# Two batches of attention back to back with their own PSUM buffers, then MLP steps alone while the third batch loads

## The chip, the cores and the metric

The kernel runs on one core of a Trainium2 chip. Its core has five instruction queues: TensorE (PE, matrix products), VectorE (DVE), ScalarE (ACT), GpSimd (POOL) and SyncE (SP). Here POOL and SP also issue the DMA transfers, POOL the loads and SP the transposing copies and the stores. PE writes into PSUM, eight banks of 128 x 512 fp32; everything else lies in SBUF. The metric is the time of one execution on the device in microseconds (us), less being better; a kernel is known by the median of its runs.

## What is computed

Attention with a decay ("forgetting") term over 8 batches of 8 heads, 576 positions, 64 features a head; its output, 4608 rows of 512, goes through an MLP whose activation is h - tanh(h). Cut to what matters:

```python
scores = np.matmul(q, k.transpose(0, 1, 3, 2)) / np.sqrt(D)      # 8 x 8 x 576 x 576
cum    = np.cumsum(np.log(np.clip(f, 0.0001, 1.0)), axis=-1)
decay  = cum[:, :, :, None] - cum[:, :, None, :]
scores = np.where(causal, -1e9, scores + decay)                  # causal: column after row
attn   = softmax(scores)
x      = np.matmul(attn, v).transpose(0, 2, 1, 3).reshape(4608, 512)
h      = x @ w_in                                                # 512 -> 2048
out    = (h - np.tanh(h)) @ w_out                                # 2048 -> 512
```

Matrix operands are fp16 (converted by the loads), sums are fp32.

## The kernel before

**Attention.** The heads go in 32 pairs (b, c): batch b, heads 2c and 2c+1. Each pair has its *slot* p = 4b + c, in which its scores are computed while the pair before gets its values. Scores are computed transposed, keys on the partitions, in seven tiles (`TILES`): three of 512 columns for each head, and one of 128 columns (`LAST`) that both heads share. A tile is one to three matmuls into a PSUM bank (L287) and an exponential on ACT into SBUF (L301), cut at the causal edge either by a matmul that adds a large negative triangle (L295, "early" slots 0 to 3) or by a select on POOL (L311). Values are 30 matmuls of 65 columns (L322), 15 a head, normalised on DVE (L332 to L334). `turn` (L338) then transposes the pair's output into `XR`, the input of the MLP: batch 0 on PE with a copy by ACT or DVE, later batches by two transposing DMAs of SP (L352, L354).

**Operands.** `QT` and `KT` hold q and k with the features on the partitions (rows 0 to 63) and three further rows that bring in the decay: constant rows (`const_rows`, L174) and rows of the cumulative logs (`load_aug`, L168), all written by SP's DMAs. There are two of each, for even and odd batches. For batches 0 and 1 q and k are loaded by `load_qk` (L84), six positions of a head in a row (1536 bytes of DRAM), turned on PE (`trans`, L242) and copied out of PSUM with a stride of 2 (L260, L262). From batch 2 on `load_block` (L89) loads blocks of 128 positions, `turn_block` (L94) turns each by a transposing DMA on SP (five for q into `TQ`, five for k into `TK`), and `place` (L98) copies the result into `QT` or `KT` on DVE. In slot 0 two tiles are computed *direct*, without the three rows, adding the decay by two matmuls with `pick_k` and `pick_q` (L290, L292).

**MLP.** 4608 rows are 9 units of 512. A unit begins with 16 steps `mlp1` (L369): four matmuls of 512 columns (`hps`, L366), tanh on ACT (L373), `gt` = h + tanh(-h) on DVE (L379). In units 1 to 8 the second product is computed as seven products of half size (`product`, L394; 14 steps of eight 256-column matmuls), which need four differences of blocks of `w_out` (`wsum`, L233) and sums of blocks of `gt` (`sums`, L383), all on DVE; `settle` (L423) adds partial results and issues the stores on SP (L435). Unit 0 takes the plain product instead, 16 steps `mlp2` (L438) of four 512-column matmuls. That is 16 + 16 + 8 x 30 = 272 steps.

**Order.** Everything is emitted in an order written out by hand, and `manual_schedule` keeps program order on all five engines. Slots 0 to 4 follow the lists `BEGIN`, `ORDER` and `THEN` (L454 to L456): s is a score tile, va and vb values, q and k transpositions for a later pair, x is `turn`, a number is so many filler matmuls (`spin`). Later slots run their seven tiles with the values after tile 1. `take` (L520) says how many MLP steps are spread over a slot: none in slots 0 to 3, 3 in slot 4, then 7 or 8. `LOADS` (L198 to L225) attaches loads, transposing DMAs and placings to a tile of a slot. What the slots leave of the MLP follows alone at the end.

**PSUM** is in four pools for the whole program: scores 2 banks (`ps_sc`), values 2 (`ps_av`), 1 shared (`ps_tr`), and 3 (`ps_m`) for the transpositions of the start and for the MLP.

Of the kernel before, what the change touches and what calls it, by code (L numbers as in the profile page):

```python
# [22 lines left out]
def kernel(  # L23
# [31 lines left out]
    aex = ctx.enter_context(tc.tile_pool(name="aex", bufs=10))  # L55
# [6 lines left out]
    ps_sc = ctx.enter_context(tc.tile_pool(name="ps_sc", bufs=2, space=PSUM))  # L62
    ps_av = ctx.enter_context(tc.tile_pool(name="ps_av", bufs=1, space=PSUM))
    ps_tr = ctx.enter_context(tc.tile_pool(name="ps_tr", bufs=1, space=PSUM))
    ps_m = ctx.enter_context(tc.tile_pool(name="ps_m", bufs=3, space=PSUM))
# [62 lines left out]
    pick_k = WS[3].rearrange("p k e -> p (k e)")[:, 0:512]  # L128
    pick_q = cst.tile([P, P], FP16)
# [4 lines left out]
    EL = [cst.tile([P, 192], FP16, tag=f"el{i}", name=f"el{i}") for i in range(3)]  # L134
    nc.vector.memset(id16, 0.0)
# [5 lines left out]
    nc.vector.memset(minus16, -1.0)  # L141
    nc.vector.memset(neg16, 0.0)
    nc.vector.memset(tri16, 0.0)
    nc.gpsimd.affine_select(out=neg16, in_=neg16, compare_op=ALU.not_equal,
# [3 lines left out]
    for i in range(2):  # L148
        nc.vector.memset(KT[i][:, :, S:PITCH], 0.0)
    nc.vector.memset(pick_k, 0.0)  # L150
    nc.vector.memset(pick_q, 0.0)
    nc.vector.memset(cqs[NH:P, :], 0.0)
    nc.vector.tensor_scalar(out=lf, in0=lf, scalar1=0.0001, scalar2=1.0,
                            op0=ALU.max, op1=ALU.min)
    nc.scalar.activation(out=lf, in_=lf, func=AF.Ln)
    nc.vector.memset(pick_k[0:1, :], -1.0)
    nc.vector.memset(pick_q[0:1, :], 1.0)
# [5 lines left out]
    nc.scalar.activation(out=cq, in_=cum, func=AF.Copy, bias=-SHIFT * inv_qscale, scale=inv_qscale)  # L163
    nc.vector.scalar_tensor_tensor(out=clo, in0=cum, scalar=inv_qscale, in1=chi,
                                   op0=ALU.mult, op1=ALU.subtract)
    nc.vector.memset(pick_k[NH:NH + 1, :], -1.0)

    def load_aug(b):  # L168
        i, h0 = b % 2, b * H
        nc.sync.dma_start(out=KT[i][D:D + 1, :, 0:S], in_=chi[h0:h0 + H, :])  # L170
        nc.sync.dma_start(out=QT[i][D + 2:D + 3, :, :], in_=cq[h0:h0 + H, :])
        nc.sync.dma_start(out=KT[i][D + 1:D + 2, :, 0:S], in_=cc[NH + h0:NH + h0 + H, :])

    def const_rows(i):  # L174
        nc.sync.dma_start(out=QT[i][D:D + 2, :, :], in_=minus16)
        nc.sync.dma_start(out=KT[i][D + 2:D + 3, :, 0:S], in_=ones16[0:H, :])

    const_rows(0)
    load_aug(0)
    const_rows(1)  # L180
    load_qk(qn, q, 0, 4, H)
    load_qk(kn, k, 0, 4, H)
    for e in EL:
        nc.gpsimd.memset(e, 0.0)
    for i in range(2):
        nc.gpsimd.memset(vn[i][D:P, NJ - 1, :, :], 0.0)
        nc.gpsimd.memset(vn[i][:, :, :, D:VW], 1.0)
    load_v(0)
# [5 lines left out]
    def load_wout(t0, t1):  # L194
# [3 lines left out]
    LOADS = {(0, 0): [lambda: load_qk(qn, q, 1, 0, 2), lambda: load_qk(kn, k, 1, 0, 2),  # L198
                      lambda: load_win(0, DFF // 2)],
             (0, 3): [lambda: load_qk(qn, q, 1, 2, H), lambda: load_qk(kn, k, 1, 2, H)],  # L200
             (1, 0): [lambda: load_v(1)],
             (1, 3): [lambda: load_win(DFF // 2, DFF)],
             (2, 0): [lambda: load_wout(0, NFT // 2)],
             (3, 0): [lambda: load_wout(NFT // 2, NFT)]}
# [4 lines left out]
    for n in range(4):  # L209
        for i in range(2):  # L210
            LOADS.setdefault((NPAIR + 3 + n, 1 + 3 * i), []).append(lambda n=n, i=i: wsum(n, i * K2 // 2, (i + 1) * K2 // 2))
    for b in range(2, B):
        p0 = (b - 1) * NPAIR
        q0, k0, v0, tq, tk = {2: (5, 10, 21, 14, 16), 3: (-2, 3, 9, 6, 12)}.get(b, (-7, 0, 7, 4, 11))
        for n in range(NJ):
            at_tile(p0, q0 + n, lambda b=b, n=n: load_block(qb, q, b, n))
            at_tile(p0, k0 + n, lambda b=b, n=n: load_block(kb, k, b, n))
            at_tile(p0, v0 + n, (lambda b=b, n=n: load_v_block(b, n, 0, H)) if n < NJ - 1 else lambda b=b: load_v_rest(b))
            at_tile(p0, tq, lambda b=b, n=n: turn_block(TQ, qb, b, n))
            at_tile(p0, tk, lambda b=b, n=n: turn_block(TK, kb, b, n))  # L220
# [16 lines left out]
    def spin(n):  # L237
        t32 = ps_tr.tile([P, UW], FP32, tag="tr", name="spin")
        for _ in range(n):
            nc.tensor.matmul(out=t32, lhsT=ones16[:, 0:P], rhs=ones16[:, 0:UW])  # L240

    def trans(b, c, src, dst, early, eng, by_head=False):  # L242
        pn, g3 = S // NT6, NT6 // 2
        if early:
            t32 = ps_m.tile([P, UW], FP32, tag="m", name="t32")
        else:
            t32 = ps_tr.tile([P, UW], FP32, tag="tr", name="t32")
        t16 = t32.bitcast(FP16)[:, 0:2 * S // 2].rearrange("p (a g n) -> p a g n", a=2, g=g3)
        for a in range(2):
            for g in range(g3):  # L250
                nc.tensor.transpose(out=t16[:, a, g, :],  # L251
# [315 lines left out]
```

## Time and profile before

| | |
|---|---|
| runs | 355.82, 356.16, 358.69 us; median 356.16 |
| the profiled execution's own time | 358.62 us |
| its span (first to last instruction in the profile) | 356.9 us |
| granted TensorE clock, mean | 0.974 |
| first scores of pair 8 (batch 2) | 74.47 us |
| last attention slot's end, MLP alone after it | about 298 us |

In the page of the profile, PE is the matmul stream and PEld its weight loads, which run beside it. A row of the chain of waits is *start, duration, engine, tile, line*; a row of a timeline the same with shapes and, in brackets, the idle time before it and what ended it. A row of a group ends in *busy us, mean ns of one, idle us before* and what ended that idle time. A row of the windows is *window, length, busy us of PE, PEld, DVE, ACT, POOL with the instructions in brackets, granted TensorE clock (1 is full), DMA share, GB/s*. SPq is SP issuing a DMA.

### The profile page before, as it was taken

How to read it: one execution, taken by the hardware profiler on the slowest of the kernel's cores; microseconds unless marked ns; L12 is line 12 of the kernel's file. 1: busy time of each engine (PE TensorE's matmuls, PEld its weight loads, DVE VectorE, ACT ScalarE, POOL GpSimd, SP SyncE). 2: the span in 40 equal slices, each digit the busy share in tenths (PEclk: the TensorE clock that was granted, in tenths of full speed). 3: DMA queues.
4: the chain of work that ended last, by engine and by line, in shares of the span. 5: the costliest groups of instructions: out<-in, count | busy, mean ns of one | idle time of the engine just before them, and what ended most of it. 6: DMA issues, size and time to landing. Idle time of an engine off the chain costs nothing.

```text
span 356.9 us, 8463 instructions
## 1 busy us (share of the span) xinstructions
PE 339.8 (95%) x3192; PEld 229.8 (64%) x3192; DVE 257.4 (72%) x501; ACT 218.8 (61%) x416; POOL 165.3 (46%) x324
## 2 busy tenths in 40 slices
PE   6698799999999999999999999999999999899995
PEld 3366455555567756887887568756887786386474
DVE  8557489963899489938893899389838855864871
ACT  6468377557775587558755875587558734533630
POOL 8941157498757755775567557753222310000000
PEclk9769889999999999999999999999999999999999
DMA  7999999999999997999799989994221112002002
GB/s 106 160 203 188 208 103 112 131 181 166 152 117 109 159 172 83 102 150 175 94 107 148 189 84 93 159 184 59 55 94 28 26 50 90 2 29 91 0 17 103
DMA packets 157469, 39.98 MB, mean 112 GB/s; under 512 B 142276, under 2 KB 155828, under 8 KB 157428
## 3 DMA queue, kind: packets, MB, share of 16 engines
q0 software_dynamic: 100128, 18.36, 70.3%
q1 hardware_dynamic: 57300, 21.09, 33.5%
q8 instruction: 25, 0.41, 0.5%
q14 instruction: 16, 0.13, 0.1%
HBM read 36.85 MB, written 9.44 MB: 130 GB/s over the span
## 4 chain that ended last, share of the span: by engine, by line
PE 79%; DVE 10%; ACT 3%; DMA 3%; SPq 2%; issue 2%; DVEq 0%; ACTq 0%
PE hps L366 29%; PE px L413 15%; PE ps L287 12%; PE pm L413 12%; PE av L322 8%; DVE gt L379 4%; PE ops L444 2%; DVE sm L392 2%; DMA QT<-cqs 2%; ACT e L301 2%; ACT th L373 2%; SPq L96 1%; DMA TK<-kn 1%; PE t L251 1%; DVE xn L334 1%
## 5 line engine op out<-in xcount | busy, mean ns | idle before, releaser
L366 PE MATMUL hps<-XR,win 128*128 128x512 f16 (+4 forms) x704 | 143.7, 344 | 2.0 <-DVE gt L379 2.0
L301 ACT ACTIVATE e<-ps 128x512 f16<-128x512 f32 x192 | 110.9, 596 | 30.5 <-PE ps L287 19.4
L373 ACT ACTIVATE th<-hps 128x512 f32<-128x512 f32 x144 | 86.3, 599 | 53.4 <-PE hps L366 47.1
L379 DVE TENSOR_TENSOR gt<-hps,th 128x512 f16<-128x512 f32 x144 | 96.7, 686 | 23.7 <-ACT th L373 22.1
L311 POOL TENSOR_SCALAR_AFFINE_SELECT e<-e 128x128 f16<-128x128 f16 x168 | 62.4, 373 | 107.8 <-ACT e L301 107.4
L366 PEld LDWEIGHTS <-win 128*128 128x128 f16 x704 | 62.4, 98 | 53.4 <-issue 7.2
L287 PE MATMUL ps<-QT,KT 67*128 67x64 f16 (+5 forms) x384 | 77.8, 285 | 5.1 <-DMA QT<-cqs 2.7
L287 PEld LDWEIGHTS <-KT 67*128 67x128 f16 (+1 forms) x384 | 37.5, 100 | 28.8 <-issue 6.4
L413 PEld LDWEIGHTS <-gt 128*128 128x128 f16 x512 | 48.0, 97 | 10.2 <-DVE gt L379 1.3
L413 PEld LDWEIGHTS <-sm 128*128 128x128 f16 x384 | 36.1, 97 | 5.4
L322 PEld LDWEIGHTS <-e 128*128 128x128 f16 x896 | 33.0, 98 | 5.6 <-issue 1.7
L322 PE MATMUL av<-vn,e 128*128 128x65 f16 x896 | 34.8, 195 | 1.3 <-DVE xn L334 1.0
L434 DVE TENSOR_TENSOR ost<-pm,part 128x512 f32<-128x512 f32 x24 | 16.5, 686 | 22.7 <-PE pm L413 8.2
L428 ACT ACTIVATE part<-px 128x512 f32<-128x512 f32 x24 | 14.3, 597 | 30.1 <-PE px L413 30.1
L413 PE MATMUL pm<-ws,gt 128*128 128x256 f16 x256 | 32.2, 272 | 0.0
L413 PE MATMUL px<-ws,sm 128*128 128x256 f16 x256 | 31.5, 272 | 0.0
L110 POOL DMA_DIRECT2D vn<-in_v_dram x32 | 28.4, 889 | 2.5 <-issue 1.4
L332 DVE TENSOR_SCALAR rs<-av 128x10 f32<-128x10 f32 (+1 forms) x33 | 5.3, 160 | 32.2 <-PE av L322 32.2
L334 DVE TENSOR_TENSOR xn<-av,rs 128x640 f16<-128x640 f32 (+1 forms) x33 | 26.5, 804 | 1.3 <-DMA out_dram<-ost 0.2
L91 POOL DMA_DIRECT2D qn<-in_q_dram x30 | 25.9, 864 | 2.1 <-issue 1.8
L91 POOL DMA_DIRECT2D kn<-in_k_dram x30 | 25.5, 849 | 1.4 <-issue 1.2
L413 PE MATMUL pm<-wout,gt 128*128 128x256 f16 x128 | 17.2, 273 | 0.2 <-DVE gt L379 0.2
(74 smaller groups left out, 291.9 us busy)
## 6 DMA issues: line engine op xcount, KB each, us to landing
out_dram<-ost SPq DMA_DIRECT2D x36, 256.0 KB
vn<-in_v_dram POOLq DMA_DIRECT2D x32, 128.0 KB, 6.3
qn<-in_q_dram POOLq DMA_DIRECT2D x24, 128.0 KB, 4.0
kn<-in_k_dram POOLq DMA_DIRECT2D x24, 128.0 KB, 5.1
win<-in_moe_w_in_dram POOLq DMA_DIRECT2D x2, 1024.0 KB, 11.8
wout<-in_moe_w_out_dram POOLq DMA_DIRECT2D x2, 1024.0 KB, 17.1
XR<-xn SPq DMA_TRANSPOSE x56
vn<-in_v_dram POOLq DMA_DIRECT2D x8, 64.0 KB, 6.9
```

The source lines that it names most:

```text
L91: nc.gpsimd.dma_start(out=dst[b % 2][0:pn, n, :].rearrange("p (h d) -> p h d", h=H), in_=src[b, :, n * P:n * P + pn, :].rearrange("h p d - ...
L110: nc.gpsimd.dma_start(out=vn[b % 2][:, n, h0:h1, 0:D], in_=v[b, h0:h1, n * P:(n + 1) * P, :].rearrange("h p d -> p h d"))
L287: nc.tensor.matmul(out=ps[:, col:col + n], lhsT=KT[b % 2][0:rows, h, j * P:(j + 1) * P], rhs=QT[b % 2][0:rows, h, i0:i0 + n], start=True, ...
L301: nc.scalar.activation(out=e[:, lo:hi], in_=ps[:, lo:hi], func=AF.Exp, scale=qscale)
L311: nc.gpsimd.affine_select(out=view, in_=view, compare_op=ALU.is_ge, fill=0.0, base=0, pattern=pat, channel_multiplier=-1)
L322: nc.tensor.matmul(out=av[:, a, ib, :], lhsT=E.pop((b, c, a, j, ib)), rhs=vn[b % 2][:, j, 2 * c + a, 0:D + 1], start=(j == 0), stop=(j == ib))
L334: nc.vector.tensor_tensor(out=xn[:, :, h0 * D:(h0 + hn) * D].rearrange("p i (a d) -> p a i d", a=hn), in0=av[:, h0:h0 + hn, :, 0:D], in1=r ...
L366: nc.tensor.matmul(out=hps[:, o:o + n], lhsT=win[:, ci, ft * P:(ft + 1) * P], rhs=XR[:, ci, t:t + n], start=(ci == 0), stop=(ci == NCH - 1))
L373: nc.scalar.activation(out=th, in_=hps, func=AF.Tanh, scale=-1.0)
L379: nc.vector.tensor_tensor(out=GT[(u, ft)], in0=hps, in1=th, op=ALU.add)
L413: nc.tensor.matmul(out=ps[:, g * E2:(g + 1) * E2], lhsT=left(k), rhs=right[:, k, :], start=(first and g == 0 and k == 0), stop=(k == K2 - ...
L434: nc.vector.tensor_tensor(out=ost, in0=ps, in1=PART.pop((u, {2: 1, 7: 5, 4: 6}[n])), op=ALU.add)
```

## The change

- **Loads.** `load_qk` takes the positions in rows of 96: the pieces are 256 bytes of DRAM, and the copies out of PSUM write runs of 96 columns instead of every second one. All loads of batches 0 and 1 (q and k in pieces of two heads), then `w_in` in four quarters and `w_out` in two halves, are issued one after the other on POOL's queue ahead of slot 0, not at tiles of slots. Batch 2's loads ("b") follow at the start of slot 7.
- **Start.** Three tiles (those of head 0) are direct; the two broadcast operands are one tile `pick` of two columns. Memsets of pads move from POOL and the prologue to DVE inside slot 0 ("p", "r"). The decay rows of batch 0 are loaded for heads 1 to 7 only, those of batch 1 in slot 0, those of batch 2 and head 0's constant rows in slot 4 ("c").
- **Slots 0 to 6.** Slot 0 has a pool of four one-bank buffers; slots 1 to 6 one of two two-bank buffers, into which tiles go in groups (0,1), (2,4), (5,6), (LAST), each with one exponential of up to 1024 columns. The transpositions alternate between two banks. No MLP step stands in these slots. Causal edges are cut by PE's matmul in slots 0 to 7. `turn` uses SP's transposing DMAs for all pairs but pair 3.
- **Slots 7 and 8.** The pools of before are opened from slot 7 on (2 banks of scores, 3 of MLP). Slot 7 holds four MLP steps among its tiles. Slot 8 starts with the values of pair 7, 18 + 12 steps alone, and batch 2's transposing DMAs and placings between them, and only then come pair 8's scores.
- **MLP.** `mlp2` and the split of a step (`mlp1_part`) are gone: all nine units take 16 + 14 steps, 270 in all. The weight differences stand in unit 0, behind its steps 14, 16, 19 and 21. From slot 8 on `take` is 5 for slots 8 to 11, 6 for 12, then 7 or 8.

SP's order after the change, from pair 7's output on: two transposing DMAs of pair 7, the store of product 2 of unit 0 (step 21), five of q, the store of product 7 (step 25), five of k.

The core of the diff:

```diff
     def load_qk(dst, src, b, h0, h1):
         nc.gpsimd.dma_start(
-            out=dst[b % 2][:, h0:h1, :, :].rearrange("p h n d -> p h (n d)"),
-            in_=src[b, h0:h1, :, :].rearrange("h (p n) d -> p h (n d)", n=NT6))
+            out=dst[b % 2][:, h0:h1, :, :].rearrange("p h n d -> p (h n) d"),
+            in_=src[b, h0:h1, :, :].rearrange("h s d -> (h s) d").rearrange("(m p) d -> p m d", p=S // NT6))
...
+    for h in (0, 2, 4):
+        load_qk(qn, q, 1, h, h + 2)
+        load_qk(kn, k, 1, h, h + 2)
+    load_v(1)
+    load_qk(qn, q, 1, 6, H)
+    load_qk(kn, k, 1, 6, H)
+    for i in (0, 2, 1, 3):
+        load_win(i * QW, (i + 1) * QW)
+    for i in range(2):
+        load_wout(i * NFT // 2, (i + 1) * NFT // 2)
...
-                to = dst[b % 2][0:D, h0:h0 + an, e:S:2].rearrange("d a (p g) -> d a p g", g=g3)
-                of = t16[e * D:(e + 1) * D, a0:a0 + an, :, :].rearrange("d a g p -> d a p g")
+                to = dst[b % 2][0:D, h0:h0 + an, 0:S].rearrange("d a (g e p) -> d a g e p", g=g3, e=2)[:, :, :, e, :]
+                of = t16[e * D:(e + 1) * D, a0:a0 + an, :, :]
...
+    GROUPS = [(0, 1), (2, 4), (5, 6), (LAST,)]
...
+        banks = POOLS["s"].tile([P, 2 if how == "group" else 1, UW], FP32, tag="sc", name="ps")
...
+        nc.scalar.activation(out=eb[:, :, lo:hi], in_=banks[:, 0:n2, lo:hi], func=AF.Exp, scale=qscale)
...
+    for at, n in ((NFT - 2, 0), (NFT, 2), (NFT + 3, 1), (NFT + 5, 3)):
+        mlp[at] += [(wsum, n, 0, K2 // 2), (wsum, n, K2 // 2, K2)]
...
+    FIRST = [["8", "q0", "k0", "5", "q1", "4", "s0", "s1", "k1", "p", "s2", "s4", "s5", "q2", "r", "s6", "s3"],
+             ["g0", "g1", "k1", "g2", "va", "vb", "q2", "x", "g3"],
+             ["g0", "va", "g1", "k1", "vb", "g2", "q2", "x", "g3"],
+             ["g0", "va", "g1", "k1", "vb", "g2", "q2", "x", "g3"],
+             ["c", "g0", "va", "g1", "k1", "vb", "g2", "x", "q2", "g3"],
+             ["g0", "g1", "k1", "g2", "va", "vb", "x", "g3"],
+             ["g0", "va", "g1", "q1", "vb", "x", "g2", "k1", "g3"],
+             ["b", "s0", "va", "s1", "vb", "m", "s2", "x", "m", "s3", "s4", "m", "s5", "m", "s6"],
+             ["va", "m", "vb", "m", "x"] + ["m"] * 16 + ["tq"] + ["m"] * 4 + ["tk"] + ["m"] * 4 + ["pq"] + ["m"] * 4 + ["pk"]]
...
+        with tc.tile_pool(name="ps_t2", bufs=1, space=PSUM) as POOLS["t"]:
+            with tc.tile_pool(name="ps_one", bufs=4, space=PSUM) as POOLS["s"]:
+                first_slot(0)
+            with tc.tile_pool(name="ps_two", bufs=2, space=PSUM) as POOLS["s"]:
+                for p in range(1, 2 * NPAIR - 1):
+                    first_slot(p)
...
+            take = 5 if p < 3 * NPAIR else 6 if p == 3 * NPAIR else 8 - p % 2
```

In `FIRST`, m is an MLP step, s a tile, g a group, tq and tk the five transposing DMAs of q and k of batch 2, pq and pk their placing.

More of the change, by code (lines that the diff above doesn't have):

```diff
@@ L303, in scores @@
             return
+        ti, e = tis[0], eb[:, 0, :]
         col, cp, step, wd = MASKS[ti]
@@ L507 @@
[L507 to L513 removed]
+    pairs = [(b, c) for b in range(B) for c in range(NPAIR)]
+    turns = [o + 2 * i + e for i in range(K2 // 2) for o in (0, K2) for e in range(2)]
@@ L536 @@
                     given += 1
-        for fn, *args in mlp[at:]:
-            fn(*args)
+        while STEPS[0] < len(mlp):
+            step()
 _INS = ['q', 'k', 'v', 'f', 'moe_w_in', 'moe_w_out']
```

403 lines of the change are left out of this document (194 added, 209 removed).

## The prediction

> **What bounds the kernel now.** I read first the page, then the windows cut at 74.47 (the start of pair 8's scores, the first of batch 2), then the chain of waits before that cut, the groups by form, and last the timelines of the start and of one early slot.
>
> ```profile
> PE 339.8 (95%) x3192; PEld 229.8 (64%) x3192; DVE 257.4 (72%) x501; ACT 218.8 (61%) x416; POOL 165.3 (46%) x324
> ...
> 0.00:74.47 74.47, 64.24 (x587) 37.50 (x587) 53.80 (x98) 45.28 (x86) 42.76 (x80) 0.89 1.38 151
> 74.47:297.78 223.31, 222.51 (x2255) 158.06 (x2256) 165.61 (x333) 149.66 (x291) 122.49 (x245) 1.00 1.17 117
> ```
>
> TensorE (PE) is 95% busy. From 74.47 on it idles 0.80 us of 223.31, so that stretch is PE work and nothing else. Of the first 74.47 us it is busy 64.24. The change rewrites that first stretch and renames work in the second, so the forecast is a forecast of when pair 8's scores start, and of how many MLP steps are done by then.
>
> ```profile
> 63.83 1.23 SPq L354
> ...
> 65.16 6.52 SPq L96 DMA_TRANSPOSE TK<-kn  x5
> 80.84 0.53 SPq L450 DMA_DIRECT2D out_dram<-ost  x1
> 81.47 6.60 SPq L96 DMA_TRANSPOSE TQ<-qn  x5
> ...
> 70.42 3.23 DMA TK<-kn
> 73.86 0.56 DVE KT L99
> 74.47 0.61 PE ps L287 x3
> 75.94 0.90 PE av L322 x30
> ...
> 87.18 0.86 PE hps L366 x4
> 108.22 0.88 PE px L413 x8
> ```
>
> The chain of waits says what starts pair 8 today: SyncE's queue (SPq) finishes the transposition of pair 7's output, issues five block transpositions of k (x5 in 6.52, so 1.30 each; 6.60 for q's five later), the last lands after 3.23, VectorE (DVE) places it (0.56), PE starts. A store costs the queue 0.53. Pair 7's values come only afterwards (0.90). Four matmuls of an mlp1 step take 0.86, eight of a product 0.88: 0.87 a step.
>
> **The exchange rate.** Before, 24 of 272 steps are done at 74.47, 248 are left, and the values. After, the slots list puts 4 steps in slot 7 and 30 in slot 8 ahead of pair 8, of 270: 236 are left and no values. That is 12 x 0.87 + 0.90 = 11.3 less. So pair 8 may start at 74.47 + 11.3 = 85.8 and the end stays where it is. All below asks whether it starts sooner.
>
> **Start (slot 0).**
>
> ```profile
> 7.46 1.99 ACT L260 ACTIVATE QT<-t 64x288 f16<-64x288 f16 x4
> 14.38 0.42 PE L287 MATMUL ps<-QT,KT 67*128 67x320 f16 x1 [2.74 <-DMA QT<-cqs]
> 18.36 0.59 PE L287 MATMUL ps<-QT,KT 67*128 67x512 f16 x1 [0.47 <-ACT e L301]
> 7.50:10.00 2.50, 1.52 (x11) 0.67 (x12) 2.41 (x5) 1.90 (x5) 2.44 (x6) 1.00 1.07 133
> 12.50:15.00 2.50, 0.62 (x5) 0.53 (x6) 0.86 (x2) 0.00 (x0) 2.50 (x5) 0.76 2.48 154
> ```
>
> PE's first scores wait for q's four copies on ScalarE (ACT), 7.46 to 9.45, and the rows of decay cost another idle 2.74 until 14.38. The change lets only head 0 go without these rows (3 tiles in place of 2) and places q1's transposition, which needs the bank that those copies free, before the scores: first scores about 9.27 + 0.9 = 10.2, the three direct tiles to 12.7, the rows (three DMAs fewer ahead of them) between 12.7 and 14.4. Slot 1 then begins at 16.5 where it began at 18.36; bounds 14.5 (rows hidden) and 18.4 (no gain). The q and k loads go from 1536-byte to 256-byte pieces. The row at 12.50 holds v's 256-byte pieces at 154 GB/s, the row at 7.50 q's long ones at 133: no loss taken.
>
> The Trainium skill, "DMA: Bandwidth & Descriptors", Specifications, puts the smallest transfer for full rate at 512 bytes; by it the new loads are slower than the old, and rival 4 below would hold. The 154 against 133 GB/s here does not agree.
>
> **Slots 1 to 6.**
>
> ```profile
> L301 ACT ACTIVATE e<-ps 128x512 f16<-128x512 f32 x192 | 110.9, 596 | 30.5 <-PE ps L287 19.4 <-PE ps L295 8.1 <-POOL e L311 1.4
> L301 ACT ACTIVATE el<-ps 128x128 f16<-128x128 f32 x32 | 8.9, 278 | 2.6 <-PE ps L287 2.1 <-PE ps L295 0.2
> L262 DVE COPY QT<-t 64x576 f16<-64x576 f16 x14 | 11.2, 800 | 4.7 <-PE t L251 4.5
> L348 DVE COPY XR<-x 128x576 f16<-128x576 f16 x1 | 0.5, 458 | 2.6 <-PE x L346 2.6
> 28.39 0.38 PE L287 MATMUL ps<-QT,KT 67*128 67x512 f16 x1
> 28.60 0.22 PE L295 MATMUL ps<-ws 128*128 128x128 f16 x1
> 28.92 0.60 ACT L301 ACTIVATE e<-ps 128x512 f16<-128x512 f32 x1 [0.41 <-PE ps L295]
> 29.94 2.52 ACT L301 ACTIVATE e<-ps 128x512 f16<-128x512 f32 x4
> 33.31 0.38 PE L287 MATMUL ps<-QT,KT 67*128 67x512 f16 x1
> ```
>
> A slot lasts 33.31 - 28.39 = 4.92 now; ACT runs four exponentials in 2.52, 0.63 each. From 128 columns (278 ns) to 512 (596) a column costs 0.83 ns, so 1024 take 0.596 + 512 x 0.83 ns = 1.02. New ACT work of a slot: 3 x 1.02 + 0.28 = 3.34. But there are two buffers of two banks: the next slot's first group (1280 columns with its two edges; 512 take 0.21 from 28.39 to 28.60, so 0.53) can be written only after the third group is read, while ACT has only the 0.28 exponential to do. With the lag from the start of PE's last write to ACT (28.60 to 28.92, 0.32) ACT idles 0.53 + 0.32 - 0.28 = 0.57, and I add 0.33 for a lag at one more group, where values stand on PE between two groups: 4.24 for slots 2, 3, 4 and 6, and 4.0 for 1 and 5, whose values come after the third group: 25.0. Ends: 3.34 and 4.92 each. DVE does not bind: its copies become contiguous (between 458 and 800 ns, near 480), four a slot, plus 1.25 for normalising: 3.2. So slot 7 begins at 16.5 + 25.0 = 41.5 (36.5 to 46).
>
> **What costs nothing here, and its cover.**
>
> ```profile
> L186 POOL MEMSET vn<- 64x528 f16 x2 | 1.3, 692 | 0.1
> L149 DVE MEMSET KT<- 67x256 uint32 x2 | 0.5, 272 | 0.0
> ```
>
> Seven memsets (three of KT, four of vn) go to DVE in slot 0, at most 3 x 0.27 + 4 x 0.69 = 3.6. They lie where DVE was busy 0.14 of 3.41 (13.80:17.21, under Clock); without that cover q2's copies, and so slot 2, would be later by as much. The transposition of pairs 0 to 2's output moves from PE and ACT to SyncE, two issues each, in an almost empty queue; the first MLP step is the first to need it, some 15 us later. Edges of slots 4 to 7 go from GpSimd to PE: eight of 128 columns, at 0.21 for 512, are 0.42 a slot, beside a bound on ACT. The 5 spins fewer are filler. Unit 0's 16 mlp2 steps of four 512-column matmuls become 14 products of eight 256-column ones, counted in the 270. Batch 3's plan moves by less than a slot, inside the stretch where PE idles 0.80.
>
> **Slot 7 and the first MLP steps.**
>
> ```profile
> L373 ACT ACTIVATE th<-hps 128x512 f32<-128x512 f32 x144 | 86.3, 599 | 53.4 <-PE hps L366 47.1 <-DVE gt L379 4.0 <-DVE rs L333 1.1
> L379 DVE TENSOR_TENSOR gt<-hps,th 128x512 f16<-128x512 f32 x144 | 96.7, 686 | 23.7 <-ACT th L373 22.1
> L392 DVE TENSOR_TENSOR sm<-gt 128x512 f16<-128x512 f16 x32 | 13.9, 435 | 1.1
> L235 DVE TENSOR_TENSOR ws<-wout 128x1024 f16<-128x1024 f16 x4 | 2.8, 706 | 0.0
> L434 DVE TENSOR_TENSOR ost<-pm,part 128x512 f32<-128x512 f32 x24 | 16.5, 686 | 22.7 <-PE pm L413 8.2 <-ACT e L301 6.3 <-issue 5.1
> 304.18 3.61 PE L366 MATMUL hps<-XR,win 128*128 128x512 f16 x16 [0.34 <-DVE gt L379]
> 40.00:45.00 5.00, 3.38 (x29) 1.86 (x28) 2.70 (x4) 1.34 (x4) 1.00 (x3) 0.84 1.24 208
> ```
>
> Slot 7 has six exponentials, the short one and four tanh on ACT: 6 x 0.63 + 0.31 + 4 x 0.63 = 6.6, so slot 8 begins at 48.1. Its values take 0.90 and the 11 steps to the fifteenth mlp1 step 11 x 0.86, with 0.34 of idle for every four (row 304.18), about 1.3 with the start: 59.8. Batch 2's loads stand behind the weights on GpSimd's queue: 3.5 MB of batches 0 and 1 at 154 GB/s is 23, 4.2 MB of weights at 208 is 20, so weights are in by 46 and batch 2 by 58. They wait for nobody and nobody waits for them.
>
> What is late is the queue of SyncE. It issues in order, and in the new order the store of product 2 (step 21) stands ahead of the five transpositions of q, the store of product 7 (step 25) ahead of the five of k. The first store waits for DVE, which after the fifteenth step's gt does, in this order, weight sums 1.41 (two of 0.71), gt 0.69, two sums 0.87, 1.41, four in-place sums 1.74, 1.41, 0.43, and the store's addition 0.69: 8.7, from 59.8 + 1.6 (tanh, gt). Store ready 70.1; q's transpositions from 70.9 to 77.5; a store 0.6; k's four spacings 5.2, landing 2.7 (the one shown 3.23, shorter when its queue is empty), wake and first copy 0.76: pair 8 at 86.8. PE gets its second weight sums (product 6) at 65.8, ends product 2 three steps later at 68.4, and then has eight products and four mlp1 steps, 10.5: it stands still some 8 us in all, part of it before the last of the four, since the gt of these steps stand behind the placing of q on DVE. Ends: 81.4 if DVE or the slots are 5 us ahead, 92 if both are behind.
>
> **Clock.**
>
> ```profile
> 10.39:13.80 3.41, 1.25 (x10) 0.51 (x7) 2.94 (x4) 1.09 (x2) 3.41 (x5) 1.00 1.96 165
> 13.80:17.21 3.41, 2.68 (x18) 1.79 (x19) 0.14 (x1) 1.73 (x3) 2.59 (x5) 0.50 2.18 157
> 34.28:37.70 3.42, 1.88 (x35) 1.30 (x32) 1.62 (x4) 2.25 (x5) 0.29 (x1) 1.00 1.17 207
> 37.70:41.11 3.41, 3.41 (x19) 1.60 (x16) 0.85 (x3) 1.19 (x2) 0.69 (x2) 0.50 1.24 210
> ```
>
> A window with PE 1.25 of 3.41 busy is followed by one at 0.50, and one with 1.88 too. After a stall of 8 us at least one window at half clock follows: 3.41/2 = 1.7 of work lost. Ends 0 and 5.1 (three windows). The same may befall slots 1 to 6, where the upper end of 46 has room for it. I take 1.7: 88.5. The Trainium skill, "TensorE: Matmul & The Clock Gate", Part 1, says half clock follows at least one idle window of about 3.4 us; since steps stand between the two gaps, by that rule nothing might be lost, and the time would be 1.7 less, 358.0; the rows here halve after windows only half idle, so I keep it.
>
> **Sum.** 88.5 - 85.8 = +2.7. Slots 8 to 11 have five steps: ACT 6 x 0.60 + 0.28 + 5 x 0.60 = 6.88 while these are mlp1, against PE's 3200 columns 1.31 + 0.90 + 5 x 0.87 = 6.56; the first 12 of the 20 steps are mlp1, two slots and a half: +0.8 (0 to 1.6). The tail (last 60 steps alone) has the same 0.34 gaps as now. Together +3.5: the span goes from 356.9 to 360.4. The profiled execution took 358.62, 2.5 above the median of the runs, 356.16; the difference is carried to the median: 359.7.
>
> **Rivals.**
> 1. *Slots at ACT's pace* (the other side: not slower). If the refill is hidden, six slots take 3.34: 5.0 less, all that follows moves with it, and the time is 354.7. It decides from about 3.5 a slot. For it: ACT's spacing in 29.94 x4 is 0.03 over its work. Against: only 0.28 of exponential covers a 0.54 refill.
> 2. *The transpositions hide.* If the queue reaches q's five before the store's wait matters, or ten pass in under 8 us, the chain ends with PE's steps at 68.4 + 10.5 = 78.9: 88.5 - 78.9 = 9.6 less, 350.1. Against: every five of these in the trace took 6.5 to 6.6, in program order.
> 3. *The wide exponential does nothing*, slots stay at 4.92: +4.1, 363.8. For: DVE or PE order, not ACT, may end the waits.
> 4. *Small pieces starve the slots.* If q and k of batches 0 and 1 come at half of 154 GB/s, their 2.4 MB take 15 us more, of which the first slots' own slack hides a third: 10 later, 369.7. The row at 12.50 speaks against.
>
> **Chances.** Forecast 0.45 (357 to 363), rival 1 0.16, rival 2 0.20, rival 3 0.14, rival 4 0.05. 1% is 3.6, about what a measurement can tell from no change: below 352.6 lie rival 2 and a little of rival 1, 0.23; within it most of rival 1 and nearly half of the forecast, 0.34; above 359.7 the rest, 0.43. The range leaves out a half of rival 2 and rival 4, 0.15, and reaches from rival 2's 350 to 3 above rival 3: 350 to 366.5.
>
> **What would show it.** Slot 1 at 16.5; slots of 4.2 with ACT idle before the first wide group; wide exponentials of 1.02; the store of product 2 issued near 70 with q's transpositions right behind it; pair 8 at 87 released by a copy of KT; PE idle 8 us before it, then a window at 0.50. It is wrong if pair 8 starts before 82, or if a load or a slot, not SyncE's queue, ends the wait.

## The result, and the profile after

The changed kernel is slower: 370.27 us median (367.73 to 371.20, four runs) against 355.99, ratio 1.038 [1.030, 1.046] (here and below the bracket is the 95% interval of the ratio to the kernel before, run beside it). Forecast were 359.7 and at most 366.5. Its profiled execution took 367.73 with a span of 366.0, the quickest of its four. ACT's timeline at the start of slot 3, two wide exponentials (1.02 each; 2.10 with what lies between), 0.70 of idle before them:

```profile
24.07 2.10 ACT L339 ACTIVATE e<-ps 128x1024 f16<-128x1024 f32 x2 [0.70 <-PE ps L323]
```

SP's timeline, then DVE's, then PE's, in the stretch ahead of pair 8:

```profile
68.85 0.43 SPq L455 DMA_DIRECT2D out_dram<-ost  x1
69.39 7.53 SPq L99 DMA_TRANSPOSE TQ<-qn  x5
77.02 0.53 SPq L455 DMA_DIRECT2D out_dram<-ost  x1
77.64 6.45 SPq L99 DMA_TRANSPOSE TK<-kn  x5
```

```profile
71.34 0.69 DVE L454 TENSOR_TENSOR ost<-mb,part 128x512 f32<-128x512 f32 x1 [0.31 <-PE mb L433]
79.71 0.69 DVE L454 TENSOR_TENSOR ost<-mb,part 128x512 f32<-128x512 f32 x1 [7.68 <-DMA out_dram<-ost]
...
86.46 0.42 DVE L415 TENSOR_TENSOR sm<-sm,gt 128x512 f16<-128x512 f16 x1
86.80 1.65 DVE L102 COPY KT<-TK 64x1152 f16<-64x1152 f16 x4
```

```profile
80.45 1.87 PE L393 MATMUL mb<-XR,win 128*128 128x512 f16 x4 [4.00 <-DVE ost L454]
82.74 1.86 PE L393 MATMUL mb<-XR,win 128*128 128x512 f16 x4 [0.42 <-DVE gt L402]
87.31 1.04 PE L323 MATMUL ps<-QT,KT 67*128 67x512 f16 x3 [2.70 <-DVE KT L102]
```

Here and below the first number of a row is its start, the second its duration. Up to here the forecast holds to little more than 1 us: the store of product 2 at 68.85 (forecast 70.1), q's five transpositions right behind it, pair 8 at 87.31 (86.8), released by a copy of `KT`. Not foreseen is DVE's 7.68 of idle: its third addition needs one of two `ost` buffers, and the store that frees it (product 7) stands in SP's queue behind q's transpositions. Nor is it foreseen that k is placed straight behind the sums (86.46), with no wait for a transfer: what holds pair 8 last is DVE's program order behind that addition. Then windows of 3.41 (PE's busy time behind the length, the granted clock third from the end), and what PE waited for from 87 to 310, behind the 2.7 for `KT` (total, times, longest):

```profile
75.24:78.65 3.41, 1.21 (x6) 0.46 (x5) 0.00 (x0) 1.19 (x2) 0.00 (x0) 1.00 1.35 151
78.65:82.06 3.41, 1.61 (x4) 0.56 (x4) 2.31 (x6) 0.00 (x0) 0.00 (x0) 0.63 0.65 141
...
85.47:88.89 3.42, 1.58 (x5) 0.64 (x6) 2.90 (x7) 0.94 (x2) 0.27 (x2) 0.50 0.43 140
88.89:92.30 3.41, 3.41 (x12) 1.47 (x11) 0.69 (x1) 1.31 (x4) 3.06 (x6) 0.50 0.73 47
92.30:95.71 3.41, 3.41 (x17) 1.53 (x16) 1.47 (x3) 2.97 (x7) 2.63 (x7) 0.87 1.45 128
95.71:99.13 3.42, 3.42 (x45) 2.07 (x44) 3.11 (x7) 2.43 (x5) 3.39 (x6) 1.00 2.44 141
```

```profile
PE mb L393 <- DVE gt L402: 2.3, 5, 0.5
PE mb L393 <- DMA XR<-xn: 1.0, 1, 1.0
PE av L360 <- POOL e L350: 0.7, 2, 0.4
```

The clock is halved from about 80 to 93, and after pair 8 three kinds of waits come, where the kernel before idled 0.80 in all up to the end of its slots. One measure carries all that follows: when pair 8 starts, and the span less that. The kernel before leaves 356.9 - 74.47 = 282.4 after it; by the exchange rate of the forecast (11.3 less work) the changed kernel should leave 271.1. It leaves 366.0 - 87.31 = 278.7.

### The profile page after: what moved, and what is told of

Read it like the earlier page. It is cut to its first block, busy times and chain, and to the rows that moved or that the text cites. A ratio compares the mean times of both kernels' runs of the same rounds, so it can differ in the third digit from the quotient of the medians.

```text
span 366.0 us, 8530 instructions
## 1 busy us (share of the span) xinstructions
PE 336.7 (92%) x3266; PEld 233.5 (64%) x3266; DVE 255.4 (70%) x523; ACT 216.2 (59%) x395; POOL 163.4 (45%) x300
## 4 chain that ended last, share of the span: by engine, by line
PE 55%; DMA 16%; DVE 10%; POOL 7%; ACT 4%; SPq 4%; issue 3%; POOLq 0%; DVEq 0%; ACTq 0%
PE mb L393 20%; PE px L433 13%; PE mb L433 10%; DMA qn<-in_q_dram 8%; PE ps L323 7%; DVE gt L402 5%; PE av L360 4%; SPq L99 3%; DVE sm L415 3%; ACT th L396 3%; DMA vn<-in_v_dram 3%; DMA kn<-in_k_dram 2%; POOL kn L88 2%; POOL vn L113 2%; ACT e L339 2%
## 5 line engine op out<-in xcount | busy, mean ns | idle before, releaser
L393 PE MATMUL mb<-XR,win 128*128 128x512 f16 (+4 forms) x704 | 145.4, 346 | 10.5 <-DVE gt L402 5.5
L339 ACT ACTIVATE e<-ps 128x512 f16<-128x512 f32 (+1 forms) x174 | 107.6, 640 | 31.2 <-PE ps L323 21.1
L402 DVE TENSOR_TENSOR gt<-mb,th 128x512 f16<-128x512 f32 x144 | 97.2, 688 | 32.3 <-ACT th L396 29.7
L396 ACT ACTIVATE th<-mb 128x512 f32<-128x512 f32 x144 | 86.2, 599 | 54.4 <-PE mb L393 39.8
L323 PE MATMUL ps<-QT,KT 67*128 67x64 f16 (+4 forms) x384 | 74.4, 280 | 7.7 <-DVE KT L102 2.7
L454 DVE TENSOR_TENSOR ost<-mb,part 128x512 f32<-128x512 f32 x27 | 18.6, 688 | 53.2 <-DMA out_dram<-ost 22.3
L323 PEld LDWEIGHTS <-KT 67*128 67x128 f16 x384 | 36.4, 99 | 26.4 <-DVE KT L102 3.6
L433 PE MATMUL mb<-ws,gt 128*128 128x256 f16 x288 | 36.0, 272 | 0.0
L368 DVE TENSOR_TENSOR xn<-av,rs 128x640 f16<-128x640 f32 x32 | 26.4, 825 | 1.1
L433 PE MATMUL mb<-wout,gt 128*128 128x256 f16 x144 | 18.7, 272 | 0.0
```

Of the source, the lines that this page charges most:

```text
L323: nc.tensor.matmul(out=ps[:, col:col + n], lhsT=KT[b % 2][0:D + 3, h, j * P:(j + 1) * P], rhs=QT[b % 2][0:D + 3, h, i0:i0 + n], start=True ...
L339: nc.scalar.activation(out=eb[:, :, lo:hi], in_=banks[:, 0:n2, lo:hi], func=AF.Exp, scale=qscale)
L368: nc.vector.tensor_tensor(out=xn.rearrange("p i (a d) -> p a i d", a=2), in0=av[:, :, :, 0:D], in1=rs.to_broadcast([P, 2, NJ, D]), op=ALU. ...
L393: nc.tensor.matmul(out=hps[:, o:o + n], lhsT=win[:, ci, ft * P:(ft + 1) * P], rhs=XR[:, ci, t:t + n], start=(ci == 0), stop=(ci == NCH - 1))
L396: nc.scalar.activation(out=th, in_=hps, func=AF.Tanh, scale=-1.0)
L402: nc.vector.tensor_tensor(out=GT[(u, ft)], in0=hps, in1=th, op=ALU.add)
```

## Experiments

The theory at this point: SP's queue makes the stall, the stall halves the clock, both add up. Rivals: the loads hold pair 8; what is gained is given back later; the two profiles compared are not typical.

**1. Both kernels again (ctl_before, ctl_after).** No edit.

> The kernel before as it is, for a second profile: the one shown took 358.62, the other runs 355.12 to 356.16. Theory A: a profile at about 355.5 has one or two windows at 0.50 fewer in the first 50 us than the one shown (which has them at 13.80 to 24.04, 37.70 and 44.52) and pair 8 at about 71.5 in place of 74.47. Rival B: the same windows, and the 3 us lie elsewhere, or in the time outside the span. Ratio 1.00.

> The changed kernel as it is. Its profiled execution took 367.73, the other three 369.53 to 371.20 at a lower mean clock (0.976 against 0.981). Theory A (the slow runs differ in how long the clock stays halved): a profile at about 370 shows more windows at 0.50 than the first one, which has them only from 78.65 to 92.3, and pair 8 at about 87 again. Rival B (they differ in the transfers): the windows at 0.50 are the same and pair 8 starts 2 to 3 later, at 89 to 90. Ratio 1.03 to 1.045 either way.

Measured: 356.01 and 369.57, ratio of the second 1.039 [1.034, 1.044]. Of the second profiles, a window and PE's row of pair 8, first of before, then of the changed kernel (spans 352.2 and 368.5):

```profile
17.21:20.63 3.42, 3.42 (x49) 3.08 (x47) 1.01 (x3) 1.63 (x3) 3.42 (x5) 0.50 1.09 194
```

```profile
69.85 0.61 PE L287 MATMUL ps<-QT,KT 67*128 67x512 f16 x3 [0.25 <-DVE KT L99]
```

```profile
41.11:44.52 3.41, 1.71 (x38) 1.38 (x36) 2.07 (x6) 1.79 (x3) 1.54 (x2) 1.00 1.22 198
44.52:47.93 3.41, 3.41 (x26) 1.84 (x23) 1.63 (x4) 1.60 (x3) 0.61 (x2) 0.52 1.25 200
```

```profile
89.92 1.03 PE L323 MATMUL ps<-QT,KT 67*128 67x512 f16 x3 [2.70 <-DVE KT L102]
```

The kernel before started pair 8 at 69.85, 4.6 sooner than in the profile of the forecast, and left 352.2 - 69.85 = 282.4, the same to a tenth. The changed kernel started it at 89.92 and left 368.5 - 89.92 = 278.6, again the same. So in these profiles each kernel varies ahead of pair 8 alone. Of the 2.6 by which the changed kernel starts it later, 1.2 lie already in slot 0 (slot 1's first exponential is at 16.62 and not 15.45, slot 7's at 43.89 and not 42.73). The other 1.4 go with a window at 0.52 in slot 7, behind one only 1.71 busy; the earlier start of before goes with about three halved windows fewer. That fits theory A's cause for a part, though pair 8 moved, as rival B had it.

**2. Fillers in the gaps (spins).** `["pq", "m", "m", "16", "m", "m", "pk", "18"]` at the end of slot 8's list.

> The changed kernel with filler matmuls in the two gaps ahead of pair 8: 16 behind the second of the four last MLP steps, 18 behind the fourth. Theory A (half clock, brought on by the gaps, costs 2.9 after pair 8 starts and about 1.5 in the steps before it): no window at 0.50 from 75 on, pair 8 at 86 to 87, span 362 to 363.5, ratio 1.02 to 1.03. Rival B (the wait for the transposed k alone is what costs): pair 8 at 87.3 or later by what filler is left over, the time within 1 us of the changed kernel, ratio 1.035 to 1.045.

Measured 371.19, 1.044 [1.038, 1.049]. The clock stays at 1.00 from 52 to 129, and nothing is won: `KT` is placed from 88.32, but the fillers run over and pair 8 starts at 89.85; what is left after it is 370.9 - 89.85 = 281.1, more than with the clock halved. PE's timeline of spins shows longer waits:

```profile
120.26 0.45 PE L360 MATMUL av<-vn,e 128*128 128x65 f16 x9 [0.32 <-POOL e L350]
130.74 0.58 PE L393 MATMUL mb<-XR,win 128*128 128x512 f16 x1 [3.60 <-DMA XR<-xn]
```

The wait for pair 11's output (`XR`, which unit 2 needs) is 3.60 where ctl_after has 1.47, and values wait for selects on GpSimd; behind the 3.60 the clock falls again (a window at 0.59 from about 130). This is rival B in substance: PE only waits longer there. As the fillers ran over, the price of half clock alone isn't isolated.

**3. The order of SP's queue (queue2), DVE's buffer (inplace), both and more (q_first).**

```diff
- ... ["m"] * 16 + ["tq"] + ["m"] * 4 + ["tk"] + ["m"] * 4 + ["pq"] + ...
+ ... ["m"] * 15 + ["tq"] + ["m"] * 5 + ["tk"] + ["m"] * 4 + ["pq"] + ...    # queue2
+ ... ["m"] * 15 + ["tq", "tk"] + ["m"] * 9 + ["pq"] + ...                   # q_first
-            nc.vector.tensor_tensor(out=ost, in0=ps, in1=PART.pop(...), op=ALU.add)
+            ost = PART.pop(...)                                             # inplace, q_first
+            nc.vector.tensor_tensor(out=ost, in0=ps, in1=ost, op=ALU.add)
```

> The changed kernel with the order of SyncE's queue alone changed: five transpositions of q, the stores of products 2 and 7, then the five of k (each step stays where it was). Theory A (the order of that queue holds pair 8 back, and with it VectorE, which waits 7.7 for the store of product 7): q's transpositions start at about 64, k's at 71 to 72, VectorE does not wait for that store, pair 8 at 81 to 83, span 360 to 362, ratio 1.01 to 1.025. Rival B (the loads hold it back: k's last block of batch 2 landed at 70.2): k's transpositions move but last longer beside the loads of v, pair 8 at 85 to 87, span 364 to 366, ratio 1.03 to 1.04.

> The changed kernel with products 2, 7 and 4 added into the tile of the partial result and stored from there, so that VectorE needs no buffer that a store has to give back; SyncE's order as in the changed kernel. Theory A (VectorE, standing 6.5 to 7.7 for the store of product 7 behind q's transpositions, is a link of its own): the wait of 7.7 is gone, q is placed about 79 to 80, the third of the four MLP steps ahead of pair 8 runs at once and not after 4.0 of idle; pair 8 then waits for k's transpositions alone, 1 to 2 earlier than in the changed kernel, less half clock: 366 to 368, ratio 1.03 to 1.04. Rival B (that wait runs beside the transpositions and costs nothing by itself): pair 8 and the time stay, ratio 1.037 to 1.045.

> As the run inplace, and the ten transpositions of batch 2 stand together ahead of all four stores of unit 0 in SyncE's order. Theory A (order of the queue and VectorE's wait together make the stall): q's transpositions from 62 to 70, k's from 71 to 77, pair 8 at 80 to 82, PE idle under 3 ahead of it and no window at 0.50 after it; against the second profile of the changed kernel (pair 8 at 89.9, 370) 8 less there and 3 less for the clock: 358 to 361, ratio 1.005 to 1.02. Rival B (loads: k's last block of batch 2 lands at 70 to 73): pair 8 at 84 to 86, 364 to 366. Rival C (given back later): pair 8 at 80 to 82, but PE then waits longer for batch 2's output at the start of unit 2 (1.0 to 1.5 now, 3.6 in the run spins): 362 to 365.

Measured: queue2 368.99, 1.035 [1.026, 1.043]; inplace 368.52, 1.037 [1.030, 1.044]; q_first 364.11, 1.024 [1.018, 1.029]. In queue2 q's transpositions went at 62.14, but DVE still waited for the store of product 7 and pair 8 started at 87.47 (SP, then DVE):

```profile
70.40 3.58 SPq L455 DMA_DIRECT2D out_dram<-ost  x2
```

```profile
80.10 0.69 DVE L454 TENSOR_TENSOR ost<-mb,part 128x512 f32<-128x512 f32 x1 [6.51 <-DMA out_dram<-ost]
```

Here that store stood ahead of k's five, issued by 73.98, and gave its buffer back 6.1 later; in the changed kernel, behind q's five, it took 2.7 (77.02 to 79.71). So order alone doesn't end the wait; what made this store slow is not shown. In inplace the wait is gone and k's placing waits 0.42 for k's transpositions; pair 8 starts at 88.35. With both, and k's five ahead of all stores, it moves (q_first, SP and PE):

```profile
62.61 7.84 SPq L99 DMA_TRANSPOSE TQ<-qn  x5
70.54 7.56 SPq L99 DMA_TRANSPOSE TK<-kn  x5
```

```profile
83.76 1.03 PE L323 MATMUL ps<-QT,KT 67*128 67x512 f16 x3 [3.23 <-DVE KT L102]
...
123.49 0.38 PE L393 MATMUL mb<-XR,win 128*128 128x512 f16 x1 [1.86 <-DMA XR<-xn]
```

Pair 8 starts at 83.76, 6.2 sooner than in ctl_after, and the median is 5.5 lower. Two links ran side by side, and mending one left the other. As q_first also has k's five ahead of the stores, the shares are not separated. 80 to 82 was expected. DVE's timeline of q_first says what holds it now:

```profile
82.38 0.42 DVE L415 TENSOR_TENSOR sm<-sm,gt 128x512 f16<-128x512 f16 x1
83.25 1.66 DVE L102 COPY KT<-TK 64x1152 f16<-64x1152 f16 x4 [0.45 <-DMA QT<-cqs]
```

As in the changed kernel, the placing of k stands behind the gt and the sums of the four MLP steps, in DVE's program order, and waits only 0.45 more for a transfer. After pair 8 there remain 278.4; of the 7 too many hardly anything is gone.

**4. Longer pieces (long) and narrow exponentials (narrow).** long restores the two lines of `load_qk` and the strided copy; narrow gives slots 1 to 6 four one-bank buffers and one exponential per tile.

> The changed kernel with the loads of q and k of batches 0 and 1 in pieces of 1536 bytes and the strided copies, as before; all else as changed. Theory A (the short pieces delay everything queued behind them on GpSimd: the weights land at 58, batch 2's k at 70 to 73): the last block of batch 2's k lands 5 or more earlier; as SyncE's order still holds pair 8, the time is only 0 to 2 less, ratio 1.03 to 1.04. Rival B (the short pieces cost no bandwidth): loads land as before within 2, and the copies of 0.80 in place of 0.47 make slots 1 to 6 longer by 0.3 to 1 each: 370 to 375, ratio 1.04 to 1.055.

> The changed kernel with exponentials of 512 columns over four one-bank buffers in slots 1 to 6, in the same order. Theory A (a wide exponential saves ACT 0.2 of 1.2 but its two buffers leave ACT idle for a refill; with four small buffers ACT works 6 x 0.60 + 0.28 = 3.88 with less idle): slots of 4.2 to 4.4, as now, the time the same within 1.5. Rival B (the wide ones are what makes the slots shorter than 4.92): slots of 4.7 to 4.9, slot 7 begins 2 to 3.5 later, and the time is 2 to 3.5 more, ratio 1.045 to 1.05.

Measured: long 375.08, 1.054 [1.049, 1.059]; narrow 368.69, 1.036 [1.031, 1.041]. Two windows (last number GB/s) and the group of the copies by form, first of long, then of the changed kernel:

```profile
13.80:17.21 3.41, 2.67 (x29) 1.88 (x30) 3.03 (x9) 2.55 (x5) 2.80 (x6) 1.00 1.30 162
...
68.41:71.82 3.41, 3.14 (x25) 2.44 (x25) 3.28 (x6) 1.53 (x3) 0.00 (x0) 1.00 0.15 10
```

```profile
L288 DVE COPY QT<-t 64x576 f16<-64x576 f16 x14 | 11.2, 802 | 1.8 <-PE t L278 1.6
```

```profile
13.80:17.21 3.41, 2.40 (x31) 1.69 (x29) 2.33 (x7) 2.55 (x5) 3.41 (x5) 1.00 2.26 135
...
68.41:71.82 3.41, 3.41 (x33) 3.06 (x32) 3.10 (x7) 0.60 (x1) 1.93 (x3) 1.00 1.88 155
```

```profile
L288 DVE COPY QT<-t 64x576 f16<-64x576 f16 x14 | 6.3, 452 | 1.9 <-PE t L278 1.8
```

Both theories of long were half right: long pieces move 162 GB/s where the short ones move 135, and the queue is empty from 68 on where it still moves 155. But the copies cost 802 in place of 452 ns, the slots grow, and pair 8 starts at 95.78; pieces and copies change together here, so their shares are not separated. The Trainium skill's line on 512 bytes ("DMA: Bandwidth & Descriptors", Specifications) agrees in direction with these windows; the forecast set it aside by comparing q with v rows of one kernel. In narrow, slots 1 to 6 last 26.3 (first exponentials 16.55 to 42.88), in ctl_after 27.3: the wide exponential brings nothing here, its refill takes what its 1.02 saves.

**5. After pair 8: three steps later against the slots (lag), batch 3's loads earlier (early3), and with q_first (e3, e3_all).**

```diff
-            take = 5 if p < 3 * NPAIR else 6 if p == 3 * NPAIR else 8 - p % 2
+            take = 5 if p < 3 * NPAIR else 3 if p == 3 * NPAIR else 8 - p % 2     # lag, e3_all
-             ["va", "m", "vb", "m", "x"] + ...
+             ["va", "m", "vb", "m", "x", "b3"] + ...      # early3, e3, e3_all: batch 3's 15 loads
```

> The changed kernel with 3 MLP steps in slot 12 in place of 6, so that all later steps come three later against the slots (63 stand alone at the end). Theory A (what is lost after pair 8 is phase: unit 2's first step comes before pair 11's output has landed, 1.0 to 1.5 of idle, and once a batch mlp1 steps meet the eight placings on VectorE, 0.45 to 0.65 of idle each): both kinds go, 3 to 4 less: 365.5 to 367, ratio 1.025 to 1.035. Rival B (they are given back elsewhere, or were not in the slower runs): within 1 of the changed kernel, ratio 1.035 to 1.045.

> The changed kernel with batch 3's fifteen loads issued on GpSimd right behind batch 2's, early in slot 8, and not among the selects of slots 8 to 10, where GpSimd is busy 3.1 to 3.4 of every 3.4. Theory A (GpSimd, with loads and selects in slots of 6.8 where it had 8.6 before, delays pair 11 and with it unit 2): the waits of values for selects and most of the wait for pair 11's output go, 1 to 2.5 less, ratio 1.03 to 1.035; pair 8 unchanged. Rival B (more loads beside the transpositions of batch 2): those take longer than 6.5 to 7.5, pair 8 comes 1 to 3 later, ratio 1.04 to 1.05.

> The run q_first (364.1) with batch 3's loads early as in early3. Theory A (GpSimd binds slots 8 to 11 once pair 8 starts sooner): 1.5 to 3 less, 361 to 362.5, ratio 1.013 to 1.02. Rival B (the loads compete with the transpositions): pair 8 later than 83.8, 364 to 367.

> As e3, with 3 steps in slot 12 as in lag, and 16 filler matmuls in the last gap ahead of pair 8 (3.2 in q_first). Theory A (half clock after the gap costs 1.7, phase 3 to 4, GpSimd 1.5 to 3, and none is given back): 355 to 358, ratio 0.997 to 1.006; no window at 0.50 or 0.75 after pair 8, no wait for pair 11's output. Rival B (given back, as in the run spins): 359 to 362, ratio 1.01 to 1.02, with a longer wait somewhere between 95 and 135.

Measured: lag 386.38, 1.085 [1.080, 1.091]; early3 374.32, 1.050 [1.043, 1.057]; e3 368.00, 1.033 [1.026, 1.039]; e3_all 364.52, 1.024 [1.018, 1.031]. Both theories of lag failed. What DVE waited for in lag from 60 to 310, then a row of PE:

```profile
DVE ost L454 <- DMA out_dram<-ost: 25.8, 4, 7.1
```

```profile
171.82 1.87 PE L393 MATMUL mb<-XR,win 128*128 128x192 f16 x8 [4.52 <-DVE ost L454]
```

and SP's timeline ahead of it:

```profile
159.90 0.53 SPq L455 DMA_DIRECT2D out_dram<-ost  x1
160.53 6.48 SPq L99 DMA_TRANSPOSE TQ<-qn  x5
167.11 1.04 SPq L455 DMA_DIRECT2D out_dram<-ost  x2
```

The link of the start is back in a later batch: the store at 167.11 stands behind five transpositions of q, DVE's next addition waits for its buffer (6.67, until 171.08), and that reaches PE: 296.3 after pair 8. Of the 17.7 more than in ctl_after, PE idles 11.1 (21.59 against 10.51); the other 6.6 are longer busy time (274.67 against 268.07), as the clock is halved behind each such wait (a window at 0.50 from about 171).

The early loads are a miss. In early3 k's five take 8.84, and above all the store of product 7, issued at 78.41, gives its buffer back late:

```profile
86.30 0.69 DVE L455 TENSOR_TENSOR ost<-mb,part 128x512 f32<-128x512 f32 x1 [12.81 <-DMA out_dram<-ost]
```

That is 6.6 later than the same addition in the first profile (79.71), and so is pair 8, at 93.95. In e3 a wait of 1.61 for a select comes. What is left after pair 8 fell in early3, to 276.5: its waits for selects are gone, and that for `XR` is 0.58. e3_all, with 276.6 after pair 8, is no better than q_first in the median.

**6. The same with DVE's wait gone (qf_spins, qf_lag, qf_all), and v's loads out of the way (qf_vlate).** Each is q_first with the named edits: 16 fillers, 3 steps in slot 12, both, and both with batch 2's loads of v in slot 8.

> The run q_first (364.1; pair 8 at 83.8 behind a gap of 3.2, then a window at 0.75) with 16 filler matmuls in that gap. Theory A (half clock after the gap is a cost of its own where no later wait takes it back): no window under 1.00 after 79, 1.5 to 2.5 less, 361.5 to 362.5. Rival B (given back, as in spins): the wait for pair 11's output near 125 grows from 1.9 by what was gained, the time within 0.8 of q_first.

> The run q_first with 3 steps in slot 12 in place of 6 (as in lag, but here VectorE waits for no store). Theory A (in the run lag the loss of 17 was VectorE waiting 4 to 7 for stores that stand behind transpositions, once in every batch; without those waits the phase itself gains): the wait for pair 11's output (1.9) and the waits for gt of 0.45 to 0.5 once a batch go, 3 to 4 less than q_first: 360 to 361. Rival B (the shift itself costs): 366 or more.

> q_first with both: filler in the gap and 3 steps in slot 12. Theory A (both gains stand, since the later wait is gone): 357.5 to 359.5, ratio 1.004 to 1.012; what is left over the kernel before is pair 8, 83.8 where 81.3 would do. Rival B: 361 to 363, one of the two is given back.

> As qf_all, with batch 2's loads of v taken out of slot 7 and put among the tiles of slot 8 (batch 3's loads and transpositions 4 or 5 tiles later). Theory A (v's loads, 8 us of traffic from 65 to 77, slow k's transpositions, which took 7.5 and landed 5 after the last where 3.2 to 3.8 were seen before): k's transpositions 6.5, pair 8 at 80.5 to 82, 355 to 357.5, ratio 0.997 to 1.007. Rival B (GpSimd's and SyncE's work of slots 8 to 11 then binds): pair 8 at 80.5 to 82, but waits of 2 to 5 between 85 and 130, 359 to 363.

Measured: qf_spins 364.35, 1.025 [1.018, 1.032]; qf_lag 362.41, 1.020 [1.015, 1.026]; qf_all 361.77, 1.018 [1.012, 1.024]; qf_vlate 372.84, 1.049 [1.043, 1.056]. So the 17 of lag were DVE's wait and the half clock behind it: without that wait the same edit costs nothing and seems to gain 1.7 (left after pair 8: 275.8), though the intervals overlap with q_first's. Fillers: 276.5 left with them against 278.4 without, as theory A has it, but they ran over, pair 8 came 1.1 later, and the median stayed; with lag 275.6 against 275.8, nothing: there PE's busy time is 1.1 shorter (265.59 against 266.69) and its idle time 0.9 longer (10.01 against 9.15). So full clock after the gap wins little here: later waits grow by nearly as much. qf_vlate, SP and PE:

```profile
70.23 6.45 SPq L99 DMA_TRANSPOSE TK<-kn  x5
```

```profile
124.28 1.03 PE L326 MATMUL ps<-QT,KT 67*128 67x512 f16 x3 [9.09 <-DVE KT L102]
```

Without v's traffic k's five take 6.45, not 7.56, but pair 8 did not come sooner: `KT` is placed from 84.02, straight behind the sums, with no wait for a transfer. So it is DVE's order, not k's transfers, that holds pair 8 there. Batch 3, moved back, arrives 9.09 late, and that is most of the 11.1 lost against qf_all.

**7. Fillers in the kernel before (b_fill, b_fill2).** `"10"` between `"s1"` and `"s2"` of `BEGIN`; in b_fill2 also 4 and 3 for 2 and 1 in `ORDER`.

> The kernel before with 10 filler matmuls (2.1 at full clock) in slot 0 where TensorE waits 1.6 to 2.7 for the decay rows. Both profiles of the kernel before show 1.25 to 1.8 busy of 3.4 there and then 1.5 to 3 windows at 0.50. Theory A (those windows cost 2 to 4, and their number makes the spread of its runs, 353.4 to 358.7): no window at 0.50 from 13.8 to 24, pair 8 at 68 to 69 (70 and 74.5 in the two profiles), 352 to 354, a spread under 2. Rival B (ScalarE paces the slots, half clock or not): the same time within 1, ratio 0.997 to 1.003.

> As b_fill, with four more fillers in each of slots 1 to 3 (0.85 a slot, where TensorE idles 0.3 to 0.5 at the slots' starts and more inside). Theory A (the clock stays full to slot 4 and the fill is hidden): at most 1 less than b_fill. Rival B (the fill lengthens slots that TensorE nearly fills): 1 to 2.5 more than b_fill.

Measured: 354.62, 0.996 [0.992, 0.999], and 354.86, 0.997 [0.993, 1.000]. b_fill still has windows at 0.67 (17.21 and 34.28) and starts pair 8 at 71.67, where its theory A had 68 to 69. b_fill2 has no window below 1.00 up to pair 8, and starts it at 71.03, later than ctl_before (69.85) with two halved ones; its runs still spread from 353.53 to 357.81. So full clock in these slots, paced by ACT, is worth some 1.4 of 356 in the median, and the windows are not the whole of what sets the two profiles of before apart. What else does is open.

## Why the prediction was wrong, by its own steps

Forecast span 360.4, profile 366.0, second profile 368.5; forecast time 359.7, median 370.27. The 10.6 between these two are:

- **Start and slots 1 to 6: right within their stated bounds, with two errors that partly cancel.** Slot 1's first exponential came at 15.45 (16.5 forecast), slot 7's at 42.73 (41.5); 25.0 was forecast for six slots and 27.3 came. The reason given for wide exponentials that gain little (ACT idles before a refill, 0.70 in the row at 24.07) was right, and narrow bears it out.
- **Pair 8's start: right to 0.5 (87.31 against 86.8), by an incomplete chain, so partly by luck** (89.92 in the second profile). SP's order was the named link, and k's landing was to end the chain; in the trace it went from the store of product 7 over DVE's third addition, the placing of q, gt and the sums to the placing of k. The steps that failed are "the gt of these steps stand behind the placing of q on DVE" (placing and gt stood behind an addition that waits for a store, 7.68; it is why queue2 won nothing sure) and "batch 2 by 58": GpSimd issued k's and v's last loads at 64.82 and 69.64,

```profile
55.53 0.87 POOL L94 DMA_DIRECT2D kn<-in_k_dram  x1 [5.35 <-DMA wout<-in_moe_w_out_dram]
...
64.82 0.69 POOL L94 DMA_DIRECT2D kn<-in_k_dram  x1 [0.31 <-issue]
...
69.64 0.70 POOL L105 DMA_DIRECT2D vn<-in_v_dram  x1
```

  as it waited behind the weights. Neither held pair 8: k's last block landed 5.8 after its issue, by about 71, before SP came to k's transpositions at 77.64. That the chain which the forecast left out ended about when its own would have ended is luck.
- **After pair 8: +5.1.** This is the mis-sized term: 1.7 for the clock and 0.8 for ACT, 273.6 in all, where 278.7 were left. Of the 7.6 over 271.1, half clock from 87.31 to 95.71 is 5.0 x 0.5 + 3.4 x 0.13 = 2.9, and PE idles 3.6 more than in the kernel before (10.47 against 6.87): 1.0 for `XR`, 0.7 for selects, the rest mostly for gt. The last 1.1 are not accounted for. The forecast looked at slots 8 to 11 for ACT alone. It missed GpSimd, busy 3.39 of 3.42 (window at 95.71) as 5 steps a slot leave less time for the same selects and loads (early3 took the waits for selects away), and missed that 34 steps spent ahead leave 26 for slots 8 to 12, so that unit 2 asks for pair 11's output as soon as it lands.
- **The reference: +5.0.** "The difference is carried to the median" failed on both sides, by 2.5 each. The profile of before was among the slowest of its runs (358.62 against 356), the first one after the quickest (367.73 against 370.3). By ctl_before, pair 8 could start at 69.85 + 11.3 = 81.2 only, not 85.8.
- **Rivals.** Rival 1 fell: slots of 27.3/6 = 4.55, not 3.34. Rival 2 (transpositions hide, 350.1) fell; q_first comes nearest. Rival 3's premise held (the wide exponential does nothing), its price did not (by the forecast's own slots it should have been 29.5 - 25.0 = 4.5, not 4.1): slots shrank anyway, with contiguous copies of 452 ns; with the strided ones of long (802) six slots last 33.1 (15.63 to 48.73). Rival 4's time, 369.7, was met by chance: the short pieces are slower, but the slots did not starve.
- **The clock rule.** The Trainium skill's rule ("TensorE: Matmul & The Clock Gate", Part 1) asks for an idle window of about 3.4 us; the forecast thought that steps between the gaps might then spare the clock. The first profile nearly agrees with the rule: the window of 1.21 shown above isn't cut where the clock changes. A mean of 0.63 in the next one puts the change near 79.5, and PE stood idle for 4.00 up to 80.45, so the 3.41 before the change hold only 0.33 of work. What speaks against the rule is ctl_after, 1.71 of 3.41 busy (41.11), then 0.52, and the forecast's own row of 1.88. Fillers that kept the clock full won nothing in the median (spins, qf_spins), but in both they ran over.

Open: 4.5 in qf_all after pair 8 (275.6 against 271.1), of which 3.1 are idle time of PE (10.01 against 6.87); what placing k ahead of the last steps on DVE would bring, which was not tried; and the spread of the kernel before. No version with the changed first stage came below the kernel before; that kernel with fillers did, by 0.4%, too little to be called faster.

## What to carry to other kernels

Measure a two-stage change by the moment where the stages meet and by what is left after it: here the second part repeated to a tenth in two profiles of the same kernel, while the total varied by 2.5 to 4.7. A transfer issued in order ahead of a store holds whoever needs the store's buffer, on another engine; mend the order and the buffer together: here either alone changed nothing clear of the noise, and a store issued first still gave its buffer back only after 6.1. Steps spent early to fill a gap are missing later, and slots made shorter need every engine's work to fit, also the one that only issues loads.

## What was not expected of the hardware

Contiguous copies out of PSUM run in 452 ns where those with a stride of 2 take 802, at 64 x 576. A window with 1.71 of 3.41 busy (ctl_after, 41.11) was followed by half clock, one with 1.80 (ctl_before, 37.69) was not. Half clock made PE's busy time 6.6 longer in lag, but where ScalarE paces the slots full clock gained under 2 of 356.
